# An attention with two dense stages on one core: U and V converted later, thresholds and copies of the first pair on GpSimd, steps moved within their slots

## The chip, the core and the metric

The kernel runs on one core of a Trainium2 chip. The metric is the device time of one launch in microseconds (us); three runs of the kernel before gave 829.96 to 831.2, median 830.89. Engines are named as in the profile: PE is TensorE, DVE is VectorE, ACT is ScalarE, POOL is GpSimd, SP issues transfers. All of them run their own queue in program order and wait for one another by semaphores.

## What is computed

```python
scores = scale * np.matmul(q, k.transpose(0, 1, 3, 2))          # 4 x 8 heads, 576 x 64
thresh = np.max(scores, axis=-1, keepdims=True) - tau
scores = np.where(scores >= thresh, scores, -1000000000.0)
attn = softmax(scores); x = attn @ v                            # heads side by side: 4 x 576 x 512
u = x + (x.transpose(0, 2, 1) @ U @ V).transpose(0, 2, 1)       # U 576 x 32, V 32 x 576
y = u + np.maximum(u @ w_ch1, 0.0) @ w_ch2                      # 512 x 2048 x 512
gate = 1 / (1 + np.exp(-causal_conv(y, conv_w)))                # 5 taps
out = gate * (y @ w_val) @ w_out
```

U, V, the weights and conv_w arrive as 64-bit floats and are turned into 32-bit floats on the chip, in about ten integer and float steps per block ("conversion").

## The kernel before

The 32 heads are worked in 16 pairs, and each pair in 9 slots of 128 query rows: slot 9p holds the 64 bottom query rows of both heads (the tail, through a block-diagonal tile `bd`), slots 9p+1 to 9p+8 the upper rows of one head or the other. A slot's row block goes through a pipeline: scores (TensorE, `s`, L429), their negated copy with the row minimum (VectorE, `ns` and `nm`, L443), the exponential (ScalarE, L457), the threshold `th = nm + tau` (L458), the mask (VectorE, `e`, L468, which needs `th` and runs one slot later), four transposes of `e` and every other slot a tail transpose (TensorE, `xm` L484 and `xs` L501, two or three slots later), their eviction (ScalarE, `pt` and `pk`). `pv` (L538) multiplies with v when a group of slots is complete: the first of pair p in slot 9p+8, the second in 9p+12. `back` (L548, L551) turns the result round and scales it into `ring`; `mix_t`, `mix_ut` and `mix_u` add the U and V product and write `u`.

The next pair is prepared meanwhile: `prep_T` (L356, L370) transposes q, k and the tails, ScalarE evicts a high part (L323, L325) and VectorE the rest (L329, L333) into `qk`; `stacks` copies them by transfers on SP into `st` (L383 to L391); `tails` copies the bottom query rows into `bd` on GpSimd (L401). Scores of slot 9 need `bd`, those of slots 10 and 11 the two `st`.

The order of each engine's queue is the order in which the program issues. A table `AT` (L198) says in which slot of its pair an event stands; `ORDER` sorts the TensorE events of a slot; evictions are put off with `later(slot, m, ...)` into four lists, which the main loop runs for m = 0 to 3, sorted by `LATE_ORDER`. A conversion is a generator (`from_f64` L100 to L131, with `wt` and `wf` as its tiles) that issues one step for each `work.tick()`, two blocks side by side; ticks come from `wtick` at point 3 of a slot, in every slot under 18 and then in the slots of `CONVERT_AT` (modulo 18), and in slots 2 to 7 at point 1 too. `setup_UV` (L651) converts U and V, from slot 0 on; its GpSimd work is `wf` (L131), the copy to `u4` (L657) and four `vst` (L666). `chunk` then converts the first weights, from slot 10. `load_qk` and `load_v` issue a pair's loads, two transfers per slot, in part on GpSimd's queue.

After 144 slots the dense stages follow; their first blocks (`a` L806, from `us` L786) are laced into the last slots. From the first `c` block on the kernel is a chain of matmuls.

Of the kernel before, what the change touches and what calls it, by code (L numbers as in the profile page):

```python
# [26 lines left out]
ALU = mybir.AluOpType  # L27
# [9 lines left out]
def attention_moe_kernel(  # L37
# [15 lines left out]
    nc = tc.nc  # L53
# [8 lines left out]
    NP = B * H // 2  # L62
# [6 lines left out]
    T = B * S  # L69
# [6 lines left out]
    def f(ap):  # L76
        return ap.bitcast(F32)
# [5 lines left out]
    tau_eff = const.tile([128, 1], F32, name="tau_eff")  # L83
    qscale = const.tile([128, 1], F32, name="qscale")
    cw = const.tile([128, KC, KD], F32, name="cw")
    u = const.tile([128, KD, T], F32, name="u")
# [90 lines left out]
    class Staged:  # L177
# [18 lines left out]


    AT = {  # L198
        "pv": (8, 12), "t": 15, "ut": 18, "u": 19, "Tq": -3, "Tk": 1, "Tt": 2, "stA": 4, "bd": 5, "stB": 5,
        "lq": 0, "lv": 4, "Tq1": 0,  # L200
    }

    ORDER = {
        "mix_t": 4, "mix_u": 3, "mix_ut": 5, "next_scores": 0, "prep_T": 5, "pv": 3, "back": 2,
        "trans_main": 2, "trans_tail": 2,
    }
    LATE_ORDER = {
        "T": 1, "n": -1, "nt": -2, "o": -1, "t": 0, "u": 1, "x": -2,
    }

    CONVERT_AT = (0, 1, 6, 9, 16)
    work = Staged(4)

    def scope():
# [11 lines left out]
    def attention(dense_front, dense_mid, dense_back):  # L226
# [18 lines left out]
        bd = [bd_p.tile([128, 2, 128], F32R, name=f"bd{i}") for i in range(2)]  # L245
# [40 lines left out]

        def load_v(p):
            b, h = divmod(2 * p, H)
            eng = nc.gpsimd if p < 4 else nc.sync
            eng.dma_start(  # L290
                out=vt[p % 2].rearrange("p h t d -> p h (t d)"),
                in_=v[b, h:h + 2, 0:SM, :].rearrange("h (p t) d -> p h (t d)", t=4),
            )
            yield
            for hh in range(2):
                eng.dma_start(out=vk[p % 2][hh * TL:(hh + 1) * TL, hh, :], in_=v[b, h + hh, SM:S, :])
                yield
# [15 lines left out]
        def later(s, k, fn, name=""):  # L313
            late[k].setdefault(s, []).append((LATE_ORDER.get(name, 0), fn))
# [134 lines left out]
        def soft_exp(p, i):  # L449
            d = st8[p]  # L450
            th = sm_p.tile([128, 1], F32, tag="th", name="th")
            if i == 0:
                d["e", 0] = e_p.tile([128, 2, S], F32, tag="e", name="e")
            elif i % 2:
                d["e", i] = d["e", i + 1] = e_p.tile([128, 2, S], F32, tag="e", name="e")
            nm = d.pop(("nm", i))
            nc.scalar.activation(out=row(p, i), in_=d["ns", i], func=ACTF.Exp, bias=nm[:, 0:1], scale=-1.0)  # L457
            (nc.gpsimd if p else nc.vector).tensor_tensor(out=th, in0=nm, in1=tau_eff, op=ALU.add)  # L458
            d["th", i] = th


# [79 lines left out]
        def back(s, p):  # L541
            d = st8[p]
            r = d["r"]
            x0, x = xtile("b0"), xtile("b")
            for g in (0, 1, 2):
                os = d.pop(("os", g))
                if not g:
                    nc.tensor.transpose(x0[0:TL, 0:128], os[:, 0:TL], idn)  # L548
                    continue
                for m in range(2 * g - 2, 2 * g):  # L550
                    nc.tensor.transpose(x[:, m * 128:(m + 1) * 128], os[:, m % 2 * 128:(m % 2 + 1) * 128], idn)  # L551
            rb = sm_p.tile([TL, 1], F32, tag="rb", name="rb")

            def act():
                nc.scalar.activation(out=rb, in_=r[TL:128, 0:1], func=ACTF.Copy)
                for hh, sc in ((0, r[0:TL, 0:1]), (1, rb)):
                    nc.scalar.activation(
                        out=x_of(p)[0:TL, 4, hh * D:(hh + 1) * D], in_=x0[0:TL, hh * D:(hh + 1) * D],
                        func=ACTF.Copy, scale=sc,
                    )  # L560

            later(s + 1, 0, act, "nt")
            later(s + 1, 2, lambda: nc.vector.tensor_tensor(
                out=x_of(p)[:, 0:4, :].rearrange("p t (h d) -> p (t h) d", h=2),
                in0=x.rearrange("p (t d) -> p t d", t=8),
                in1=r[:, 1:9].unsqueeze(2).to_broadcast([128, 8, D]), op=ALU.mult,
            ), "n")
# [39 lines left out]
        for hh in range(2):  # L607
            t = st8[0]["st", hh] = st_p.tile([128, 3, S], F32R, tag="st", name="st")
# [4 lines left out]
        for m in range(2):  # L613
# [7 lines left out]
            out=rv[0][:, 0:8 * R].rearrange("p (t r) -> p t r", t=4),  # L621
# [30 lines left out]
        def setup_UV(part):  # L652
            w = yield from convert(raw_uv[part])
            o = 0 if part else nu
            c, n = (FC - nu, nu + S - FC) if part else (0, FC - nu)
            if not part:
                nc.gpsimd.tensor_scalar(  # L657
                    out=u4.rearrange("p t (g r) -> p t g r", g=4),
                    in0=w[:, 0:nu].rearrange("p (t r) -> p t r", t=5).unsqueeze(2).to_broadcast([128, 5, 4, R]),
                    scalar1=1.0, scalar2=0.0, op0=ALU.mult, op1=ALU.add,  # L660
                )
            nc.scalar.activation(out=vst[:, c:c + n], in_=w[:, o:o + n], func=ACTF.Copy)
            yield
            for a in (R, 3 * R):
                lo = vst[a:a + R, c:c + n]
                nc.gpsimd.tensor_tensor(out=lo, in0=w[a:a + R, o:o + n], in1=f(lo), op=ALU.subtract)  # L666
            done.append(0)

        NS = 9 * NP + AT["ut"] - 7
        slots = [[] for _ in range(NS + 2)]  # L670
        def put(s, what, *a):
            slots[s].append((what, a))

        for p in range(NP):
            s0 = 9 * p
            for i in range(9):
                put(s0 + i + 2, trans_main, p, i)
                if i % 2 == 0:
                    put(s0 + i + 2 + (i == 8), trans_tail, p, i)
            put(s0 + AT["pv"][0], pv, p, 0, 1)  # L680
            end = p == NP - 1
            put(s0 + AT["pv"][1], pv, p, 2)
            put(s0 + AT["pv"][1] + 2, back, p)
            if p + 1 < NP:
                s1 = s0
                put(s1 + AT["Tq" if p else "Tq1"], prep_T, p + 1, "q")
                put(s1 + AT["Tk"], prep_T, p + 1, "k")
                put(s1 + AT["Tt"], prep_T, p + 1, "tail")
                put(s1 + AT["stA"], stacks, p + 1, 0)
                put(s1 + AT["bd"], tails, p + 1)  # L690
                put(s1 + AT["stB"], stacks, p + 1, 1)
            put(s0 + AT["t"], mix_t, p)
            put(s0 + AT["ut"] - end, mix_ut, p)
            put(s0 + AT["u"] - 2 * end, mix_u, p)
        def next_scores(s):
            scores(*divmod(s + 1, 9))

        last = (stacks, tails)
        work.add(setup_UV(0))
        work.add(setup_UV(1))  # L700
        scores(0, 0)
        for s in range(NS):
            p, i = divmod(s, 9)
            slot[0] = s
            live = p < NP
            ev = slots[s]
            if s == 10: chunk(0, 0)
            if s == 10: chunk(0, 1)
            work.width = 2 if s < 9 * NP - 11 else 4
            def wtick(at):  # L710
                if at == 3 and (s < 18 or s % 18 in CONVERT_AT) or at == 1 and 2 <= s < 8:
                    work.tick()
            wtick(-1)
            if live:
                soft_max(p, i)
            for m in (0, 1, 2, 3):
                for _, fn in sorted(late[m].pop(s, []), key=lambda x: x[0]):
                    fn()
                if m == 1 and live:
                    soft_exp(p, i)  # L720
                if m == 2 and 1 <= s <= 9 * NP:
                    soft_mask(*divmod(s - 1, 9))
                wtick(m)
            wtick(4)
            if s + 1 < 9 * NP:
                ev = [(next_scores, ())] + ev
            for what, a in sorted(ev, key=lambda x: 9 if x[0] in last else ORDER.get(x[0].__name__, 5)):
                what(*a) if what in last else what(s, *a)
            if i == AT["lq"] and p + 2 < NP:
                loads.append(load_qk(p + 2))  # L730
            if i == AT["lv"] and p + 1 < NP:
                loads.append(load_v(p + 1))
            load(2)
            if s == 9 * NP:
                front.close()
                ps_s.close()
            if s == 9 * NP + 1:
                mid.close()
                dense_mid()
            if s == 9 * NP + AT["pv"][1] + 2 - 9:  # L740
                top.close()
            if s >= 9 * NP:
                steps = next(dense_front, None)
                if s == 9 * NP:
                    later(s + 1, 0, lambda: list(steps))
                work.tick()
# [304 lines left out]
```

## Time and profile before

| | |
|---|---|
| median of three runs | 830.89 us |
| profiled execution | 831.23 us, span 829.5 us |
| PE (TensorE) busy | 815.3 us, 98% |
| DVE (VectorE) busy | 616.2 us, 74% |
| ACT (ScalarE) busy | 437.4 us, 53% |
| POOL (GpSimd) busy | 240.3 us, 29% |
| chain that ended last | PE 90%, ACT 4%, DMA 2%, POOL 2%, DVE 1% |

The chain is followed back from the last instruction, at each step to what released it or to the instruction ahead of it on its engine. A busy TensorE can still be slower than it need be: matmul ends are modelled, and a matmul that waits for its data inside a run of matmuls counts as busy. A share over the whole span also mixes the attention (about 324 us) with the dense stages.

### The profile page before, as it was taken

Reading aid. Unit: us, or ns where it says so; the run is one execution under the profiler, and the core shown is the slowest. Engines: PE = TensorE matmul, PEld = TensorE weight load, DVE = VectorE, ACT = ScalarE, POOL = GpSimd, SP = SyncE. Lnnn points to the kernel's source line nnn. Section 1 sums busy time; section 2 is a strip of 40 time slices with the busy share of each in tenths; the row PEclk is TensorE's granted clock in tenths of the full one; section 3 lists DMA queues with packets and bytes.
Section 4 is the critical chain, followed back from the end, with each engine's and each line's share of the span. In section 5 each row is a group of like instructions: output and inputs, shape, how many; then the busy total and the mean of one; then the engine's idle time right before and its main releaser. Section 6 shows DMA issues by size and latency. Waiting matters only on the chain.

```text
span 829.5 us, 14295 instructions
## 1 busy us (share of the span) xinstructions
PE 815.3 (98%) x5084; PEld 691.9 (83%) x5084; DVE 616.2 (74%) x1309; ACT 437.4 (53%) x894; POOL 240.3 (29%) x329
## 2 busy tenths in 40 slices
PE   8799999999999999999999999999999999999998
PEld 7688888888888887788888888888888888888886
DVE  7799898999889898356874776357743688999740
ACT  5588888888878888223333232224222334345431
POOL 6744543364334332002430352005220233200000
PEclk9999999999999999999999999999999999999999
DMA  5655586667766540001220221003110111001112
GB/s 134 166 145 130 135 197 143 148 145 171 167 145 151 147 101 27 2 18 59 76 77 1 75 77 52 1 3 101 51 51 1 52 51 51 1 1 51 51 51 76
DMA packets 63567, 68.07 MB, mean 82 GB/s; under 512 B 43349, under 2 KB 46821, under 8 KB 63498
## 3 DMA queue, kind: packets, MB, share of 16 engines
q1 hardware_dynamic: 60730, 63.68, 29.5%
q0 software_dynamic: 1424, 3.10, 1.2%
q8 instruction: 41, 0.67, 0.3%
q10 hardware_dynamic: 1344, 0.39, 0.2%
q14 instruction: 28, 0.23, 0.1%
HBM read 35.89 MB, written 4.72 MB: 49 GB/s over the span
## 4 chain that ended last, share of the span: by engine, by line
PE 90%; ACT 4%; DMA 2%; POOL 2%; DVE 1%; issue 1%; SPq 0%; ACTq 0%; DVEq 0%; POOLq 0%
PE c L806 24%; PE a L806 24%; PE s L429 8%; PE o L538 8%; PE v L806 6%; PE p L965 6%; PE xm L484 6%; PE t L577 2%; PE o L527 2%; ACT pt L493 1%; PE tm L356 1%; ACT e L457 1%; PE u L589 1%; PE xs L501 1%; DMA st<-qk 1%
## 5 line engine op out<-in xcount | busy, mean ns | idle before, releaser
L806 PE MATMUL a<-us,w 128*128 128x512 f32 (+1 forms) x960 | 202.3, 369 | 0.6 <-DVE us L786 0.6
L806 PE MATMUL c<-h,w 128*128 128x512 f32 (+1 forms) x960 | 200.7, 368 | 0.0
L806 PEld LDWEIGHTS a<-us,w 128*128 128x128 f32 x960 | 167.0, 189 | 31.5 <-DVE us L786 1.3
L806 PEld LDWEIGHTS c<-h,w 128*128 128x128 f32 x960 | 167.4, 189 | 30.0
L817 ACT ACTIVATE h<-a 128x512 fp32r<-128x512 f32 (+1 forms) x80 | 44.2, 554 | 186.9 <-PE a L806 186.9
L131 POOL TENSOR_TENSOR wf<-wf,wt 128x512 f32<-128x512 f32 (+2 forms) x43 | 58.5, 1361 | 268.2 <-DVE wt L126 268.2
L458 POOL TENSOR_TENSOR th<-nm,tau_eff 128x1 f32<-128x1 f32 x135 | 80.7, 598 | 165.9 <-DVE ns L443 164.5
L818 DVE SCALAR_TENSOR_TENSOR h<-a,h 128x512 fp32r<-128x512 f32 (+1 forms) x80 | 50.8, 636 | 103.6 <-ACT h L817 103.6
L443 DVE TENSOR_SCALAR_CACHE_REDUCE ns<-s 128x576 f32<-128x576 f32 x144 | 108.3, 752 | 19.8 <-PE s L429 19.7
L468 DVE SCALAR_TENSOR_TENSOR e<-ns,th,e 128x576 f32<-128x576 f32 x144 | 119.5, 830 | 0.7 <-ACT e L457 0.5
L457 ACT ACTIVATE e<-ns,nm 128x576 f32<-128x576 f32 x144 | 111.5, 774 | 13.3 <-DVE ns L443 12.9
L429 PE MATMUL s<-st 128*128 128x288 f32 x480 | 94.0, 318 | 0.0
L493 ACT ACTIVATE pt<-xm 128x512 f32<-128x512 f32 x144 | 85.4, 593 | 5.7 <-PE xm L484 3.1
L484 PE MATMUL xm<-idn,e 128*128 128x128 f32 x576 | 86.7, 274 | 0.7 <-DVE e L468 0.7
L429 PEld LDWEIGHTS s<-st 128*128 128x128 f32 x480 | 67.8, 189 | 11.5 <-issue 4.6
L484 PEld LDWEIGHTS xm<-idn,e 128*128 128x128 f32 x576 | 69.9, 141 | 1.6 <-ACT pk L515 0.6
L538 PE MATMUL o<-pt,vt 128*64 128x256 f32 (+1 forms) x768 | 69.8, 331 | 0.0
L538 PEld LDWEIGHTS o<-pt,vt 128*64 128x64 f32 x768 | 41.4, 137 | 24.5 <-issue 10.6
L172 POOL TENSOR_TENSOR w<-wf,w 128x512 fp32r<-128x512 f32 x36 | 54.5, 1530 | 10.0 <-ACT w L170 10.0
L871 DVE TENSOR_TENSOR y<-c,y 128x64 f32<-128x64 f32 (+4 forms) x96 | 39.8, 449 | 21.2 <-PE c L806 21.2
L894 DVE SCALAR_TENSOR_TENSOR u<-y,cw,u 128x576 f32<-128x576 f32 x64 | 55.0, 872 | 0.6
L786 DVE TENSOR_TENSOR us<-u,us 128x1024 fp32r<-128x1024 f32 (+1 forms) x42 | 47.7, 1176 | 7.2 <-ACT us L785 7.2
(122 smaller groups left out, 1035.7 us busy)
## 6 DMA issues: line engine op xcount, KB each, us to landing
raw<-in_moe_w_ch_dram SPq DMA_DIRECT2D x32, 512.0 KB, 3.9
st<-qk SPq DMA_DIRECT2D x30, 256.0 KB, 3.4
st<-qk SPq DMA_DIRECT2D x15, 432.0 KB, 4.0
st<-qk SPq DMA_DIRECT2D x45, 144.0 KB, 3.4
out_dram<-ring SPq DMA_DIRECT2D x17, 256.0 KB, 2.0
st<-qk SPq DMA_DIRECT2D x15, 288.0 KB, 4.8
kn<-in_k_dram SPq DMA_DIRECT2D x28, 128.0 KB, 3.4
qn<-in_q_dram SPq DMA_DIRECT2D x26, 128.0 KB, 3.5
```

Of the source, the lines that this page charges most:

```text
L131: nc.gpsimd.tensor_tensor(out=dst, in0=dst, in1=tf, op=ALU.add)
L172: lo_eng.tensor_tensor(out=lo, in0=w, in1=f(hi), op=ALU.subtract)
L429: nc.tensor.matmul(s[:, n, 0:HS], lhs, rhs[:, n * HS:(n + 1) * HS], start=(m == 0), stop=(m == len(ops) - 1))
L443: nc.vector.tensor_scalar(out=ns.rearrange("p (a b) -> p a b", a=2), in0=s, scalar1=-1.0, scalar2=3.0e38, op0=ALU.mult, op1=ALU.min, accum ...
L457: nc.scalar.activation(out=row(p, i), in_=d["ns", i], func=ACTF.Exp, bias=nm[:, 0:1], scale=-1.0)
L458: (nc.gpsimd if p else nc.vector).tensor_tensor(out=th, in0=nm, in1=tau_eff, op=ALU.add)
L468: nc.vector.scalar_tensor_tensor(out=e, in0=d.pop(("ns", i)), scalar=d.pop(("th", i))[:, 0:1], in1=e, op0=ALU.is_le, op1=ALU.mult, accum_o ...
L484: nc.tensor.transpose(x[:, j * 128:(j + 1) * 128], e[:, c + j * 128:c + (j + 1) * 128], idn)
L493: later(s + 1, 0, lambda: nc.scalar.activation(out=dst, in_=x.rearrange("p (j c) -> p j c", j=4), func=ACTF.Copy), "x")
L538: nc.tensor.matmul(o, lhs, rhs, start=False, stop=stop)
L806: nc.tensor.matmul(ps[:, 0:m1], lhs, rhs, start=(m == 0), stop=(m == len(ops) - 1))
L894: nc.vector.scalar_tensor_tensor(out=g, in0=y[:, e, b, k:k + S], scalar=cw[:, k, e:e + 1], in1=g, op0=ALU.mult, op1=ALU.add)
```

## The change

What it does, in the order of the diff:

- `AT`, `PREP_AT`: `back` stands in slot 13 of its pair (14 before), `mix_u` in 18 (19 before), the odd tail transpose (i = 8) a slot sooner; the `bd` copies stand in slot 4 of the pair that runs while they are prepared (5 before).
- `LATE_ORDER`: evictions of `prep_T` come first in their list (they came last, together with those of `u`).
- `CONVERT_AT`: six slots in eighteen, five before; the tick moves from point 3 of a slot (behind list 3) to point 0 (behind list 0).
- v of pairs 0 to 3 is loaded through SP, not GpSimd.
- The thresholds of pair 0 are computed on GpSimd as all others are; they were on VectorE.
- U and V enter the conversion at slot 4, not at slot 0.
- The mask is issued at the end of list 1, ahead of lists 2 and 3; `ring` moves from list 2 to list 1.

```diff
     AT = {
-        "pv": (8, 12), "t": 15, "ut": 18, "u": 19, "Tq": -3, "Tk": 1, "Tt": 2, "stA": 4, "bd": 5, "stB": 5,
-        "lq": 0, "lv": 4, "Tq1": 0,
+        "pv": (8, 12), "back": 13, "t": 15, "u": 18, "lq": 0, "lv": 4, "uv": 4, "ch": 10,
     }
+    PREP_AT = {"Tq": (-3, 0), "Tk": (1, 1), "Tt": (2, 2), "stA": (4, 4), "bd": (4, 4), "stB": (5, 5)}
...
     LATE_ORDER = {
-        "T": 1, "n": -1, "nt": -2, "o": -1, "t": 0, "u": 1, "x": -2,
+        "T": -2, "n": -1, "nt": -2, "o": -1, "t": 0, "u": 1, "x": -2,
     }
-    CONVERT_AT = (0, 1, 6, 9, 16)
+    CONVERT_AT = (0, 1, 6, 9, 12, 16)
...
         def load_v(p):
-            eng = nc.gpsimd if p < 4 else nc.sync
+            eng = nc.sync
...
-            (nc.gpsimd if p else nc.vector).tensor_tensor(out=th, in0=nm, in1=tau_eff, op=ALU.add)
+            nc.gpsimd.tensor_tensor(out=th, in0=nm, in1=tau_eff, op=ALU.add)
...
-            later(s + 1, 2, lambda: nc.vector.tensor_tensor(
+            later(s + 1, 1, lambda: nc.vector.tensor_tensor(
                 out=x_of(p)[:, 0:4, :].rearrange("p t (h d) -> p (t h) d", h=2),
...
                 if i % 2 == 0:
-                    put(s0 + i + 2 + (i == 8), trans_tail, p, i)
+                    put(s0 + i + 2, trans_tail, p, i)
...
-            put(s0 + AT["pv"][1] + 2, back, p)
+            put(s0 + AT["back"] + end, back, p)
...
-            put(s0 + AT["ut"] - end, mix_ut, p)
-            put(s0 + AT["u"] - 2 * end, mix_u, p)
+            put(s0 + AT["u"] - end, mix_ut, p)
+            put(s0 + AT["u"] - end, mix_u, p)
...
-        work.add(setup_UV(0))
-        work.add(setup_UV(1))
         scores(0, 0)
...
+            if s == AT["uv"]:
+                work.add(setup_UV(0))
+                work.add(setup_UV(1))
...
             def wtick(at):
-                if at == 3 and (s < 18 or s % 18 in CONVERT_AT) or at == 1 and 2 <= s < 8:
+                if at == 0 and (s < 18 or s % 18 in CONVERT_AT) or at == 1 and 2 <= s < 8:
                     work.tick()
...
-                if m == 1 and live:
-                    soft_exp(p, i)
-                if m == 2 and 1 <= s <= 9 * NP:
-                    soft_mask(*divmod(s - 1, 9))
+                if m == 1:
+                    if live:
+                        soft_exp(p, i)
+                    if 1 <= s <= 9 * NP:
+                        soft_mask(*divmod(s - 1, 9))
                 wtick(m)
```

The queues show what moves. In the changed file the lines from L200 on are one higher. First GpSimd (POOL), from the end of pair 2's loads to the first threshold of pair 1; `wf`, `u_120` and `vst` are the U and V conversion, `bd_126` the copies for pair 1, `th` the thresholds. Before:

```order
L281 DMA tn<-in_q_dram 64x2x64
L131 TENSOR_TENSOR wf<-wf,wt 128x512
L657 TENSOR_SCALAR u_120<-wf 128x640
L131 TENSOR_TENSOR wf<-wf,wt 128x224
L281 DMA tn<-in_k_dram 64x2x64
L290 DMA vt_130<-in_v_dram 128x2x256
L666 TENSOR_TENSOR vst<-wf,vst 32x352 x2
L666 TENSOR_TENSOR vst<-wf,vst 32x224 x2
L401 TENSOR_SCALAR bd_126<-qk 64x64 x4
L296 DMA vk_132<-in_v_dram 64x64 x2
L458 TENSOR_TENSOR th<-nm,tau_eff 128x1
```

And in the changed kernel, from the copies to threshold 10:

```order
L402 TENSOR_SCALAR bd_126<-qk 64x64 x4
L282 DMA tn<-in_k_dram 64x2x64
L459 TENSOR_TENSOR th<-nm,tau_eff 128x1 x2
L131 TENSOR_TENSOR wf<-wf,wt 128x512
L459 TENSOR_TENSOR th<-nm,tau_eff 128x1
L658 TENSOR_SCALAR u_120<-wf 128x640
L131 TENSOR_TENSOR wf<-wf,wt 128x224
L667 TENSOR_TENSOR vst<-wf,vst 32x352 x2
L459 TENSOR_TENSOR th<-nm,tau_eff 128x1
L667 TENSOR_TENSOR vst<-wf,vst 32x224 x2
L459 TENSOR_TENSOR th<-nm,tau_eff 128x1
L277 DMA qn<-in_q_dram 128x4x64 x2
```

The copies stand ahead of the conversion, and thresholds 7, 8 and 9 stand inside it; threshold 10 follows the two loads.

Second VectorE (DVE), slots 1 to 3 of pair 0. Before:

```order
L468 SCALAR_TENSOR_TENSOR e,sum<-ns,th,e 128x576
L329 SCALAR_TENSOR_TENSOR qk<-tm,qscale,qk 128x512
L105 TENSOR_SCALAR wt<-wt 128x512
L443 TENSOR_SCALAR ns,nm<-s 128x576
L458 TENSOR_TENSOR th<-nm,tau_eff 128x1
L108 TENSOR_SCALAR wt<-wt 128x512
L105 TENSOR_SCALAR wt<-wt 128x224
L468 SCALAR_TENSOR_TENSOR e,sum<-ns,th,e 128x576
L333 TENSOR_TENSOR qk<-tm,qk 128x512
L112 SCALAR_TENSOR_TENSOR wf<-raw,wt 128x512
L108 TENSOR_SCALAR wt<-wt 128x224
L443 TENSOR_SCALAR ns,nm<-s 128x576
```

And now:

```order
L469 SCALAR_TENSOR_TENSOR e,sum<-ns,th,e 128x576
L330 SCALAR_TENSOR_TENSOR qk<-tm,qscale,qk 128x512
L444 TENSOR_SCALAR ns,nm<-s 128x576
L469 SCALAR_TENSOR_TENSOR e,sum<-ns,th,e 128x576
L334 TENSOR_TENSOR qk<-tm,qk 128x512
L444 TENSOR_SCALAR ns,nm<-s 128x576
```

Thresholds and conversion steps are gone from here; the conversion steps come back between mask 3 and mask 6.

Third ScalarE (ACT), slots 16 and 17, where the first weight block (`wt<-raw`) is converted and pair 2's q is evicted (`qk<-tm`). Before:

```order
L578 ACTIVATE t_st_127<-t 128x128
L323 ACTIVATE qk<-tm,qscale 128x512
L457 ACTIVATE e<-ns,nm 128x576
L103 ACTIVATE wt<-raw 128x512
L493 ACTIVATE pt<-xm 128x4x128
```

And now:

```order
L579 ACTIVATE t_st_127<-t 128x128
L103 ACTIVATE wt<-raw 128x512
L324 ACTIVATE qk<-tm,qscale 128x512
L458 ACTIVATE e<-ns,nm 128x576
L494 ACTIVATE pt<-xm 128x4x128
```

The conversion step stands ahead of the eviction instead of behind the exponential.

## Rows read from the trace of the kernel before

**Rows 1.** Windows by stage: start and end, length, busy us of each engine, PEclk, DMA share, GB/s.

```profile
0.00:40.00 40.00, 31.71 (x231) 28.13 (x232) 29.10 (x80) 21.02 (x43) 26.52 (x48) 0.96 0.60 156
40.00:320.00 280.00, 279.01 (x2386) 239.88 (x2384) 254.66 (x678) 239.49 (x559) 116.89 (x213) 1.00 0.60 143
354.00:829.50 475.50, 471.62 (x2285) 398.69 (x2283) 315.39 (x524) 161.88 (x261) 92.73 (x65) 1.00 0.14 45
```

**Rows 2.** Timeline of TensorE, 30 to 54 us: start, length, instruction, idle before.

```profile
31.83 1.89 PE L429 MATMUL s<-qk,bd 128*128 128x288 f32 x6 [2.97 <-POOL bd L401]
...
34.58 1.10 PE L527 MATMUL o<-pk,vk 128*128 128x64 f32 x4
...
39.56 0.60 PE L484 MATMUL xm<-idn,e 128*128 128x128 f32 x4
...
41.08 0.60 PE L484 MATMUL xm<-idn,e 128*128 128x128 f32 x4
...
42.28 0.60 PE L484 MATMUL xm<-idn,e 128*128 128x128 f32 x4
...
51.66 1.04 PE L429 MATMUL s<-qk,bd 128*128 128x288 f32 x6
52.53 0.60 PE L484 MATMUL xm<-idn,e 128*128 128x128 f32 x4
...
53.08 1.10 PE L527 MATMUL o<-pk,vk 128*128 128x64 f32 x4
```

**Rows 3.** Window of 1 us behind the idle stretch, columns as in rows 1.

```profile
32.00:33.00 1.00, 1.00 (x4) 0.96 (x5) 0.00 (x0) 0.00 (x0) 0.94 (x3) 0.50 0.89 348
```

**Rows 4.** Timeline of VectorE, 20 to 40 us; then its thresholds, grouped by line.

```profile
27.47 0.75 DVE L443 TENSOR_SCALAR_CACHE_REDUCE ns<-s 128x576 f32<-128x576 f32 x1
...
28.34 0.81 DVE L468 SCALAR_TENSOR_TENSOR e<-ns,th,e 128x576 f32<-128x576 f32 x1
...
38.78 0.76 DVE L443 TENSOR_SCALAR_CACHE_REDUCE ns<-s 128x576 f32<-128x576 f32 x1 [3.06 <-PE s L429]
...
39.47 0.81 DVE L468 SCALAR_TENSOR_TENSOR e<-ns,th,e 128x576 f32<-128x576 f32 x1
...
L458 DVE TENSOR_TENSOR th<-nm,tau_eff 128x1 f32<-128x1 f32 x9 | 2.2, 242 | 0.3
```

**Rows 5.** Timeline of GpSimd, 20 to 40 us.

```profile
21.19 1.26 POOL L131 TENSOR_TENSOR wf<-wf,wt 128x512 f32<-128x512 f32 x1 [7.10 <-DVE wt L126]
...
23.33 1.15 POOL L131 TENSOR_TENSOR wf<-wf,wt 128x224 f32<-128x224 f32 x1
...
25.86 4.53 POOL L666 TENSOR_TENSOR vst<-wf,vst 32x352 fp32r<-32x352 f32 x4
...
35.28 1.56 POOL L276 DMA_DIRECT2D qn<-in_q_dram  x2
```

**Rows 6.** Thresholds on GpSimd, 30 to 320 us: shortest, median, longest in ns.

```profile
L458 POOL TENSOR_TENSOR th<-nm,tau_eff x134: 188/637/792, 34.7 to 318.2; 128x1 f32<-128x1 f32 x134
```

**Rows 7.** SP's queue, first and last stack transfer; then landing times, 0 to 50 us.

```profile
20.58 0.52 SPq L383 DMA_DIRECT2D st<-qk  x1
...
27.98 0.85 SPq L391 DMA_DIRECT2D st<-qk  x1
...
st<-qk SPq DMA_DIRECT2D x5, 144.0 KB, 4.9
```

**Rows 8.** Chain that ended last, 60 to 130 us: first `pv` of pairs 2 to 4.

```profile
73.31 2.34 PE o L538 x32
...
92.67 2.34 PE o L538 x32
...
111.77 2.34 PE o L538 x32
```

**Rows 9.** Timeline of TensorE, 324 to 333 us: the hand-over to the dense stage.

```profile
325.85 3.06 PE L806 MATMUL a<-us,w 128*128 128x512 f32 x11 [0.57 <-DVE us L786]
...
332.28 0.70 PE L527 MATMUL o<-pk,vk 128*128 128x256 f32 x2 [0.52 <-ACT pk L515]
```

More of the change, by code (lines that the diff above doesn't have):

```diff
@@ L667, in setup_UV @@
             done.append(0)
-        NS = 9 * NP + AT["ut"] - 7
-        slots = [[] for _ in range(NS + 2)]
+        NS = 9 * NP + AT["u"] - 7
+        slots = [[] for _ in range(NS + 1)]
         def put(s, what, *a):
@@ L675, in attention @@
             s0 = 9 * p
+            end = p == NP - 1
             for i in range(9):
@@ L678, in attention @@
                 if i % 2 == 0:
-                    put(s0 + i + 2 + (i == 8), trans_tail, p, i)
+                    put(s0 + i + 2, trans_tail, p, i)
             put(s0 + AT["pv"][0], pv, p, 0, 1)
-            end = p == NP - 1
             put(s0 + AT["pv"][1], pv, p, 2)
-            put(s0 + AT["pv"][1] + 2, back, p)
+            put(s0 + AT["back"] + end, back, p)
             if p + 1 < NP:
[L685 to L691, printed above, removed]
+                for name, what, *a in (("Tq", prep_T, "q"), ("Tk", prep_T, "k"), ("Tt", prep_T, "tail"),
+                                       ("stA", stacks, 0), ("bd", tails), ("stB", stacks, 1)):
+                    put(s0 + PREP_AT[name][not p], what, p + 1, *a)
             put(s0 + AT["t"], mix_t, p)
-            put(s0 + AT["ut"] - end, mix_ut, p)
-            put(s0 + AT["u"] - 2 * end, mix_u, p)
+            put(s0 + AT["u"] - end, mix_ut, p)
+            put(s0 + AT["u"] - end, mix_u, p)
         def next_scores(s):
@@ L706, in attention @@
             ev = slots[s]
-            if s == 10: chunk(0, 0)
-            if s == 10: chunk(0, 1)
+            if s == AT["uv"]:
+                work.add(setup_UV(0))
+                work.add(setup_UV(1))
+            if s == AT["ch"]:
+                chunk(0, 0)
+                chunk(0, 1)
             work.width = 2 if s < 9 * NP - 11 else 4
             def wtick(at):
-                if at == 3 and (s < 18 or s % 18 in CONVERT_AT) or at == 1 and 2 <= s < 8:
+                if at == 0 and (s < 18 or s % 18 in CONVERT_AT) or at == 1 and 2 <= s < 8:
                     work.tick()
@@ L739, in attention @@
                 dense_mid()
-            if s == 9 * NP + AT["pv"][1] + 2 - 9:
+            if s == 9 * NP + AT["back"] + 1 - 9:
                 top.close()
```

## The prediction

> **What bounds the kernel now.** I read the stage windows first. From 354 us to the end TensorE works back to back: 471.62 of 475.50 us busy, and the rest is the last output's way out. From 40 to 320 us it is busy for 279.01 of 280 us. Only the first 40 us have air: 31.71 us busy, 8.3 us idle [rows 1]. So a change to the attention's order can win some microseconds at the start, little in the middle, and what the hand-over to the dense part near 325 us loses; nothing after that.
>
> Next the TensorE timeline of the first pair [rows 2]. The scores of slot 9 (the `bd` block) start at 31.83 us after 2.97 us of waiting for GpSimd's four `bd` copies; the first `pv` follows at 34.58. The reader should set beside it the same piece one pair later: scores 51.66, transposes 52.53, `pv` 53.08. It takes 1.42 us there and 2.75 us here. The reason stands in the windows: behind the idle stretch the granted clock is 0.50, that is 1.2 in place of 2.4 GHz [rows 3]. Wait and half clock together cost 2.97 + 1.33 = 4.3 us.
>
> Then VectorE in the same stretch [rows 4]. Its rows name no wait, it works through: mask 6 ends at 28.34 + 0.81 = 29.15. The transposes of mask 6 stand right behind the `bd` scores, so without the `bd` wait VectorE would be next.
>
> **The change, part by part.** All sums are against the profiled execution, 831.23 us (span 829.5), which lies 0.34 us above the median of 830.89; I take the gain from the median.
>
> *Thresholds of pair 0 to GpSimd.* With its threshold a slot spends 28.34 - 27.47 = 0.87 us from the start of `ns` to the mask, without it 39.47 - 38.78 = 0.69 [rows 4]. Eight of the nine stand before mask 6: 8 x 0.18 = 1.4 us at least; the nine were busy for 2.2 us, since some were held up, and that is the most. I take 2.0, nearer to the busy time, which is measured in this very stretch. The conversion of U and V stays ahead of mask 6 on VectorE (it only starts at slot 4), so nothing else goes from this sum: mask 6 ends near 27.1. Transposes and tail take 53.08 - 52.53 = 0.55 us, so the first `pv` starts near 27.7 in place of 34.58: 6.9 us. That holds the 4.3 us of wait and half clock.
>
> *`bd` copies in slot 4, ahead of U and V on GpSimd.* They read the tails that VectorE evicts in slot 3, and are through well before the scores of slot 9. The wait of 2.97 us goes; its gain is in the 6.9.
>
> *What is late next: GpSimd.* In its new queue the U/V work stands between the thresholds 6 and 9, and the loads of pair 3 behind threshold 9. VectorE ends the wide `wt` some 2.0 us before mask 6 (mask 0.81, `ns` 0.69 and two narrow steps), at 25.1. From there GpSimd needs 24.48 - 21.19 = 3.29 us for both `wf` and the copy between, 4.53 us for four `vst`, 1.56 us for two loads of q, and the thresholds 7 to 10 [rows 5]. A threshold took 0.188 to 0.792 us there, median 0.637 [rows 6]. Before, TensorE came to the transposes of masks 8, 9 and 10 at 39.56, 41.08 and 42.28 us, 4.98, 6.50 and 7.70 us after `pv` [rows 2]; from 27.7 that is 32.7, 34.2 and 35.4.
> With every threshold at 0.64 us: `wf` and threshold 7 to 29.1, two `vst` to 31.4, threshold 8 to 32.0, its mask to 32.8 (0.1 late); two `vst` and threshold 9 to 34.9, mask to 35.7 (1.4 late); loads and threshold 10 to 37.1, mask to 37.9 (1.0 late). In sum 2.5 us lost.
> With thresholds 8 to 10 at 0.19 us the masks end at 32.4, 34.9 and 36.6: 0 + 0.7 + 0.5 = 1.2 us lost. VectorE waits for these thresholds with nothing to run, so the short value may well hold; but the long one is the median. I take 1.8, the middle. Start: 6.9 - 1.8 = 5.1 us.
>
> The median of 0.64 us beside a shortest of 0.19 is what a threshold shows that lies behind a mask [rows 6]. The Trainium skill, SBUF — State Buffer, section Who interferes with whom, says that a VectorE instruction with two SBUF inputs and a GpSimd instruction that reads SBUF shut each other out for the length of the one that came first. By that rule moving thresholds to GpSimd only moves the contention, but not in slots 8 to 10, where masks wait: there the short times hold, and the sum would be 7.5 us in place of 6.9. The trace agrees so far as the two durations show.
>
> *The stacks' transfers.* SP issues nine transfers from 20.58 to 28.83 us, and 144 KB took 4.9 us to land in this stretch [rows 7]. One `vt` load now stands among them; at an estimated 0.8 us (the last stack took 0.85) the last lands 8.25 + 0.8 + 4.9 = 14.0 us after the tails are evicted. The scores of slot 11, which stand right ahead of the transposes at 32.7, want it by 32. So the tails must be out by 18, 2.6 us sooner than before. Four thresholds no longer stand ahead of them (0.7 us), nor do the seven conversion steps of the first slots: I estimate 3 us together and cost this at nothing. If only the thresholds counted, it would cost 1.9 us, and that is in the range. `vt` and `vk` of pair 0 on SP: nothing, they are issued at the start.
>
> *Conversion early in a slot, `T` evictions first, `back` and `tail` a slot sooner.* Pairs alternate between 111.77 - 92.67 = 19.10 and 92.67 - 73.31 = 19.36 us [rows 8]; where it is 19.36 the chain runs through ScalarE ahead of `pv` (`qk`, exponential, a conversion step, `pt`). In the new order that conversion step stands ahead of `qk`, where ScalarE had to wait for the transposes anyway. Four or five odd pairs show it: 0.26 x 4 = 1.0 at best, nothing at worst. I take 0.8. A conversion step between `ns` and the mask delays a mask by up to a step; masks have a slot of slack there, so 0.
>
> *One more conversion slot in eighteen.* The steps of chunk 0 end before the last slots, and none is left between the last masks and `us`. TensorE waits 0.57 us for `us` at 325.85 and 0.52 us for `pk` at 332.28, which lies on ScalarE behind such a step [rows 9]. The last tail transpose also comes ahead of the `a` block now. Both can go: 1.1 at best, 0.4 if one stays; I take 1.0.
>
> Sum: 5.1 + 0.8 + 1.0 = 6.9 us. From 830.89 that gives **824.0 us**.
>
> **The rivals.** 0.2% (1.7 us) is about what a measurement of this kernel can tell from no change.
>
> *GpSimd costs nothing.* Thresholds and `vst` run at their short times, `pv` starts at 27.3 (the whole 2.2 us of thresholds saved), the odd pairs lose all their excess: 7.3 + 1.0 + 1.1 = 9.4 us, 821.5 us. For it: VectorE waits in that stretch and holds nobody up. Against: two loads of 1.56 us stand ahead of threshold 10 whatever VectorE does.
>
> *GpSimd costs more.* The `bd` copies and loads make thresholds late in slots 4 to 6 too, and the masks there lie on VectorE's full queue: 1 to 2 us more lost, odd pairs keep their excess: 6.9 - 2.0 - 0.8 = 4.1 us, 826.8 us. For it: a threshold in GpSimd's queue waits for loads of 0.78 us each. Against: a threshold has a whole slot until its mask.
>
> *The wait only moves.* In place of `bd` the scores of slot 11 wait for the stacks' transfers, or the late thresholds eat the start's gain; 5 us lost again: within 1.7 us of before, 829.2 to 832.5. Against: the transfers start with the tails, which come earlier.
>
> *Slower.* GpSimd becomes the bound from slot 7 to 11. Nine instructions (two `wf`, the copy, four `vst`, two thresholds) each wait for one more mask of 0.81 us than in their rows: 7.3 us; TensorE idles in stretches as long as the one before and drops to half clock again, 1.3 us. 6.9 - 7.3 - 1.3 = -1.7: 832.6 us. It decides from the point where GpSimd's stretch grows by 7 us. Against: masks that wait for thresholds can't hold them up as well.
>
> **How the numbers follow.** My forecast has 0.62 with its own range of 822.3 to 826.0; GpSimd for nothing 0.14; GpSimd dearer 0.14; the wait only moves 0.06; slower 0.04. The first three are all faster by over 1.7 us: 0.90. The range runs from the best case with half a microsecond of doubt, 821.0, to the dearer case with 1.2 us, 828.0.
>
> **What would show it.** Right: no `bd` wait; `pv` of pair 0 at 27 to 28.5 us; clock 1.00 from 20 to 40 us; masks 9 and 10 waiting for thresholds, 1 to 2.5 us of TensorE idle between 31 and 38 us; pair periods all near 19.1; no wait for `us` or `pk` near 325. Wrong: `pv` of pair 0 after 30 us, a wait for `st`, or a half clock anywhere.

## The result, and the profile after

The changed kernel takes **820.47 us** (median of four runs, 820.41 to 820.97), beside 830.93 us for the kernel before (829.96 to 831.2) in the same batch: 10.46 us less, ratio 0.9877 with a 95% interval of 0.986 to 0.9895. The forecast was 824.0 us with a range of 821.0 to 828.0, so the sign was right and the gain was under-sized by 3.5 us, half a microsecond beyond the range. Most runs of the kernel before lie near 829.4 or near 831.1 us, and its median moves between these from batch to batch; a gain is therefore given against the median of its own batch, and where a microsecond matters it is read from the traces.

The windows by stage of the changed kernel, columns as in [rows 1], which they answer to:

```profile
0.00:40.00 40.00, 36.47 (x281) 31.74 (x282) 34.35 (x88) 26.86 (x57) 29.47 (x61) 1.00 0.65 169
40.00:320.00 280.00, 278.23 (x2402) 240.84 (x2400) 260.37 (x679) 241.74 (x563) 101.48 (x200) 1.00 0.61 143
320.00:345.00 25.00, 25.00 (x129) 20.11 (x128) 8.42 (x12) 8.13 (x17) 0.16 (x1) 1.00 0.00 1
```

The first 40 us hold 4.8 us more of TensorE's work, and the clock is full throughout. TensorE's busy time in the middle has not risen; it has even fallen from 279.01 to 278.23 us, and yet the middle is shorter. That is the riddle of this case.

TensorE's timeline at the first pair, which answers to [rows 2]:

```profile
25.21 1.02 PE L430 MATMUL s<-qk,bd 128*128 128x288 f32 x6 [0.81 <-DVE ns L444]
26.68 0.63 PE L485 MATMUL xm<-idn,e 128*128 128x128 f32 x4 [0.45 <-DVE e L469]
27.15 0.27 PE L502 MATMUL xs<-idn,e 128*128 128x128 f32 x1
27.26 0.92 PE L528 MATMUL o<-pk,vk 128*128 128x64 f32 x4
```

The wait for `bd` is gone, the scores of slot 9 take 1.02 us and not 1.89, and the first `pv` starts at 27.26 us, 7.32 sooner than before. From there I took the start of every pair's first `pv` and that of the dense stage's `c` block, and how much sooner each comes than before: pair 0 7.32 us, pair 1 6.57, pair 5 7.38, pair 9 8.98, pair 15 8.83, the `c` block 10.45 (343.54 in place of 353.99). So 0.75 us of the start is lost in the first period, 2.3 us are won in the middle, 1.6 at the hand-over to the dense part.

### The profile page after: what moved, and what is told of

The parts are those of the page before. It is cut to its first block, busy times and chain, and to the rows that moved or that the text cites. A ratio compares the mean times of both kernels' runs of the same rounds, so it can differ in the third digit from the quotient of the medians.

```text
span 818.7 us, 14233 instructions
## 1 busy us (share of the span) xinstructions
PE 809.9 (99%) x5084; PEld 690.2 (84%) x5084; DVE 617.7 (75%) x1300; ACT 437.4 (53%) x894; POOL 223.8 (27%) x326
## 4 chain that ended last, share of the span: by engine, by line
PE 94%; DVE 2%; ACT 2%; DMA 1%; issue 1%; POOL 0%; SPq 0%; ACTq 0%; POOLq 0%; DVEq 0%
PE a L806 24%; PE c L806 24%; PE s L430 9%; PE o L539 8%; PE xm L485 7%; PE v L806 6%; PE p L965 6%; PE o L528 2%; PE t L578 2%; PE tm L357 1%; PE xs L502 1%; PE u L590 1%; DMA kn<-in_k_dram 1%; PE b L552 1%; DVE e L469 1%
## 5 line engine op out<-in xcount | busy, mean ns | idle before, releaser
L469 DVE SCALAR_TENSOR_TENSOR e<-ns,th,e 128x576 f32<-128x576 f32 x144 | 124.3, 863 | 1.5 <-POOL th L459 0.4
L459 POOL TENSOR_TENSOR th<-nm,tau_eff 128x1 f32<-128x1 f32 x144 | 72.4, 503 | 175.1 <-DVE ns L444 168.1
L172 POOL TENSOR_TENSOR w<-wf,w 128x512 fp32r<-128x512 f32 x36 | 54.0, 1514 | 10.0 <-ACT w L170 10.0
```

The lines of the kernel that those rows point to most:

```text
L172: lo_eng.tensor_tensor(out=lo, in0=w, in1=f(hi), op=ALU.subtract)
L459: nc.gpsimd.tensor_tensor(out=th, in0=nm, in1=tau_eff, op=ALU.add)
L469: nc.vector.scalar_tensor_tensor(out=e, in0=d.pop(("ns", i)), scalar=d.pop(("th", i))[:, 0:1], in1=e, op0=ALU.is_le, op1=ALU.mult, accum_o ...
```

## The experiments

Each was timed beside the kernel before in its own batch. Where a run is set against the changed kernel (820.47 us), the two medians come from different batches; the traces, given beside them where it matters, differ from that by about half a microsecond at most. "Period" is the time from one pair's first `pv` to the next pair's.

**The start alone, in the kernel before.**

```
-  eng = nc.gpsimd if p < 4 else nc.sync
+  eng = nc.sync
-  (nc.gpsimd if p else nc.vector).tensor_tensor(out=th, ...
+  nc.gpsimd.tensor_tensor(out=th, ...
-  put(s1 + AT["bd"], tails, p + 1)
+  put(s1 + (AT["bd"] if p else 4), tails, p + 1)
+  if s == 4: work.add(setup_UV(0)); work.add(setup_UV(1))
```

> The kernel before with the start alone changed: U and V converted from slot 4, the first pair's thresholds on GpSimd, the bottom queries of pair 1 copied in slot 4, the first v loads on SP. Theory A (start worth 7.3, GpSimd's late thresholds cost 0.9): 6.4 us, 824.0 to 825.0 us, the first pv near 27.3 us and pair periods 19.10 and 19.36 as before. Theory B (GpSimd's queue costs the 1.8 us that the prediction took, and the chunk's conversion steps that come sooner help the later pairs): first pv the same but over 25.5 us from it to the last pair, 825.3 to 826.3 us.

Measured: 825.90 us (825.82 to 826.82) beside 831.04, 5.1 us less. The first `pv` starts at 27.54 us, 7.04 sooner; the first period is 20.51 us and not 18.50, 2.0 us lost; the later ones are those of before (19.33, 19.10, 19.39, 19.13). Theory B's price holds, without its help to later pairs: the prediction's start, 6.9 - 1.8 = 5.1 us, is right in its sum and nearly in both terms. So the missing gain is not at the start.

The 2.0 us are not lost where the prediction put them, though, at the late masks 8 to 10. The rows of GpSimd, ScalarE (two) and TensorE show the larger part:

```profile
26.09 1.86 POOL L131 TENSOR_TENSOR wf<-wf,wt 128x512 f32<-128x512 f32 x1
27.99 0.50 ACT L662 ACTIVATE vst<-wf 128x352 fp32r<-128x352 f32 x1 [1.39 <-POOL wf L131]
28.39 0.58 ACT L493 ACTIVATE pt<-xm 128x512 f32<-128x512 f32 x1
29.02 0.70 PE L527 MATMUL o<-pk,vk 128*128 128x256 f32 x2 [1.04 <-ACT pt L493]
```

ScalarE's copy of V into `vst` waits for GpSimd's `wf`, a `pt` stands behind that copy, and TensorE stops inside the first `pv` until that `pt` is done (1.04 us under PE, 1.18 under the weight loads). By the program the first `pv` does not read this `pt`, whose rows belong to the second; so it must be the PSUM tile that it waits for, as mix_t does further down. Of the masks only one stops TensorE: mask 10, whose threshold stands behind two loads, for 0.7 us at 36.93.

**`back` in slot 13 alone, in the kernel before.**

```
-  put(s0 + AT["pv"][1] + 2, back, p)
+  put(s0 + AT["pv"][1] + 1 + end, back, p)
```

> The kernel before with one edit: the back transposes stand in slot 13 of a pair and not in slot 14 (the last pair keeps 14). Theory A: the missed microseconds in the middle are mix_t's wait of 0.28 us in each of 15 pairs, which ends with the eviction of `back`; a slot sooner it goes, so 15 x 0.28 = 4.2 us at most: 826.5 to 828.0 us, with the wait of the t weight load gone from the list of waits and periods of about 18.85 us. Theory B (the conversion steps early in a slot make the middle faster): this edit alone does nothing, 830.4 to 831.4 us.

Measured: 825.82 us (825.23 to 826.89) beside 831.04, ratio 0.9943 (0.993 to 0.9955): 5.2 us less, more than theory A allowed, and theory B falls. In the trace the periods go from 19.10 and 19.36 to 18.79 and 19.06, 0.3 us each, and from pair 0 to pair 15 it is 4.6 us; the rest of this run's gain lies ahead of the first `pv` and is told at the end. TensorE's weight loads (PEld) in pair 6 of the kernel before show what went; the columns are start, length, instruction, idle before:

```profile
163.66 0.50 PEld L484 LDWEIGHTS xm<-idn,e 128*128 128x128 f32 x4
164.12 0.14 PEld L501 LDWEIGHTS xs<-idn,e 128*128 128x128 f32 x1
164.54 1.19 PEld L577 LDWEIGHTS t<-ring,u 128*128 128x128 f32 x10 [0.28 <-ACT pt L493]
```

The first weights of mix_t wait 0.28 us. ScalarE's timeline names the place:

```profile
163.27 0.20 ACT L555 ACTIVATE rb<-r 64x1 f32<-64x1 f32 x1
163.50 0.31 ACT L557 ACTIVATE ring<-b,r 64x64 f32<-64x64 f32 x1
163.72 0.30 ACT L557 ACTIVATE ring<-b,rb 64x64 f32<-64x64 f32 x1
163.91 0.58 ACT L493 ACTIVATE pt<-xm 128x512 f32<-128x512 f32 x1
```

The three evictions of `back` stand ahead of that `pt`, which ends at 164.49; mix_t starts 0.05 us later, in this pair and in all fifteen. One line of the list of waits sums it up (total, times, longest):

```profile
PEld t L577 <- ACT pt L493: 4.3, 15, 0.3
```

In the kernel with `back` in slot 13 that line is absent, and so it is in the changed kernel, where the same piece reads:

```profile
156.26 0.14 PEld L502 LDWEIGHTS xs<-idn,e 128*128 128x128 f32 x1
156.37 1.20 PEld L578 LDWEIGHTS t<-ring,u 128*128 128x128 f32 x10
```

The window of the middle in the kernel with `back` in slot 13, to be set beside the second row of [rows 1]:

```profile
40.00:320.00 280.00, 278.97 (x2420) 241.69 (x2419) 258.57 (x683) 240.73 (x566) 120.59 (x212) 1.00 0.61 142
```

PE is busy for 278.97 us, as before for 279.01, though each pair takes 0.3 us less. In pair 6 of the kernel before the `xs` matmul ahead of mix_t counts as busy from 164.23 to 164.50 us, although its weights were in by 164.26 and mix_t's began at 164.54: the wait lies inside a busy time. Only the number of instructions (2420 in place of 2386) and PEld's busy time (241.69 in place of 239.88) say that more was done. The Trainium skill, Perfetto Trace Analysis, section Identifying the Most-Contended Engine, says that the busy share of matmuls is no measure of how near TensorE is to its limit and that of the weight loads is; these two rows agree.

**`back` put back to slot 14, in the changed kernel.**

```
-  put(s0 + AT["back"] + end, back, p)
+  put(s0 + AT["back"] + 1, back, p)
```

> The changed kernel with `back` put back to slot 14, all else as changed. Theory A: mix_t waits again, 820.5 + 3.0 to 4.2 = 823.5 to 824.7 us. Theory B: 820.0 to 821.2 us.

Measured: 825.13 us (824.87 to 825.53), 4.7 us above the changed kernel, 0.4 more than theory A allowed: its direction holds and theory B falls. mix_t waits again; most periods are 19.1 to 19.2 us in place of 18.8 to 18.9. But the 4.7 us are not that wait alone. In twelve pairs mix_t waits 0.3 to 0.4 us as before, 3.6 us in sum; in the other three it waits 0.98, 1.16 and 1.18 us, and there it is the ring that is late, since a conversion step of VectorE stands ahead of its eviction. In return three other waits of the changed kernel, told below, do not come here.

**mix_t moved away instead, in the kernel before.**

```
-  put(s0 + AT["t"], mix_t, p)
+  put(s0 + AT["t"] + 1 - end, mix_t, p)
```

> The kernel before with `back` left in slot 14 and mix_t moved from slot 15 to slot 16 instead (the last pair keeps 15). Theory A (all that counts is that a whole slot lies between the ring evictions of `back` and mix_t, so that TensorE finds ScalarE's and VectorE's evictions done): the wait of 0.28 us in 15 pairs goes here too, 4.2 to 4.6 us less than before, 825.3 to 826.8 us. Theory C (the gain came from what else moved with `back`, its ScalarE evictions ahead of other pt evictions): nothing, 829.4 to 831.3 us.

Measured: 838.80 us (837.66 to 839.2) beside 829.40, 9.4 us slower. Both expectations are wrong, and the weight loads say why. What now stands where mix_t stood, the transposes `tm` of the next queries, waits in its place:

```profile
166.57 0.14 PEld L501 LDWEIGHTS xs<-idn,e 128*128 128x128 f32 x1
167.01 0.42 PEld L356 LDWEIGHTS tm<-idn,qn 128*128 128x128 f32 x4 [0.30 <-ACT pt L493]
```

`tm` reads nothing of the ring. So the wait of the kernel before was not for the ring: it belongs to the place in the order, the third PSUM tile that is drawn in slot 15 (after `xm` and `xs`). The pool has four such tiles (L239), and the third one drawn there begins 0.05 us after ScalarE has read slot 14's `xm`, whoever draws it. That the pool hands it the very buffer of that `xm` is inferred from this; the trace names no buffers. And the next user of mix_t's own tile pays more. From the list of the weight loads' waits of this kernel:

```profile
PEld o L527 <- DVE t_st L579: 8.8, 15, 1.4
...
PEld tm L356 <- ACT pt L493: 3.8, 13, 0.3
```

`pv`, in the next slot, waits until VectorE has read t: 8.8 us in 15 pairs, where the kernel before has no such line. By the same inference moving `back` ahead is good because its two tiles are drawn and read a slot sooner: then whoever comes third in slot 15 gets a tile that was read long ago.

**The conversion steps where they were, in the changed kernel.**

```
-  CONVERT_AT = (0, 1, 6, 9, 12, 16)
+  CONVERT_AT = (0, 1, 6, 9, 16)
-  if at == 0 and (s < 18 or s % 18 in CONVERT_AT) ...
+  if at == 3 and (s < 18 or s % 18 in CONVERT_AT) ...
```

(the mask and the ring eviction also go back to the later part of the slot)

> The changed kernel with the conversion steps where they were: at the end of a slot, in five slots of eighteen, and mask and back eviction in their old part of the slot. Theory A (the steps early in a slot give the odd pairs' 0.26 us and the tail about 1.0, and cost three stretched masks of 0.57 us each): the three stalls go (-1.7), the odd pairs' excess and the tail's waits return (+2.0 to +3.0): 820.8 to 822.0 us. Theory B (they make the whole gain of the middle, 2.3 us, and the tail's 1.6): 823.5 to 825.0 us.

Measured: 821.70 us (821.19 to 821.76), 1.2 us above the changed kernel. By the trace that is three things: the first `pv` and the first period together take 48.13 us and not 46.51 (1.6 us more), from pair 1 to pair 15 it is 263.11 and not 264.46 (1.35 us *less*), and from there to the `c` block 33.44 and not 32.57 (0.9 more). So the early steps, with the sixth slot and the earlier mask and ring eviction that go with them, help at both ends and hurt in the middle. At the start ScalarE's wait for `wf`, seen in the run with the start alone, is here too (1.04 us under PE at 29.52) and is gone in the changed kernel, whose `wf` begins at 24.28 us. In the middle the excess of every other period (19.06 against 18.81) is back, as forecast; but the three long periods of the changed kernel, 19.57, 19.87 and 19.46 us (those that end with the first `pv` of pairs 4, 10 and 14), are 19.26, 18.80 and 18.56 us here.

**The ring eviction behind the mask, in the changed kernel.** In those three periods a mask takes 1.68 us. VectorE's timeline of the first of them, then GpSimd's, then TensorE's:

```profile
97.00 0.69 DVE L564 TENSOR_TENSOR ring<-b,r 128x512 f32<-128x512 f32 x1
97.60 1.68 DVE L469 SCALAR_TENSOR_TENSOR e<-ns,th,e 128x576 f32<-128x576 f32 x1
```

```profile
97.24 0.19 POOL L459 TENSOR_TENSOR th<-nm,tau_eff 128x1 f32<-128x1 f32 x1
97.38 1.28 POOL L172 TENSOR_TENSOR w<-wf,w 128x512 fp32r<-128x512 f32 x1
```

```profile
99.43 0.63 PE L485 MATMUL xm<-idn,e 128*128 128x128 f32 x4 [0.57 <-DVE e L469]
```

GpSimd's step of slot 6 waits for nothing of slot 6, so GpSimd runs ahead to it as soon as slot 5's threshold is out. Slot 5 is the one in which VectorE evicts the ring between `ns` and the mask: in that gap GpSimd begins a pass of 1.28 us, and the mask that comes 0.22 us later is held. The edit closes the gap:

```
-  later(s + 1, 1, lambda: nc.vector.tensor_tensor(
+  later(s + 1, 2, lambda: nc.vector.tensor_tensor(
       out=x_of(p)[:, 0:4, :]...
```

> The changed kernel with one instruction per pair moved on VectorE: the eviction of `back` into the ring stands behind the mask of its slot and not between `ns` and the mask. Theory A: the three masks of 1.68 us (pairs 4, 10 and 14) are held out by GpSimd's conversion step of 1.28 us, which GpSimd runs ahead to as soon as the slot's threshold is out, because the ring eviction of 0.69 us leaves it the gap; with the mask right behind `ns` they go back to 0.81 and the periods of 19.57, 19.87 and 19.46 us to about 18.85: 0.72 + 1.02 + 0.61 = 2.3 us less, 818.0 to 818.9 us. Theory B: the masks are long because VectorE's own conversion steps crowd slot 6; moving the ring eviction does nothing, 820.1 to 821.0 us.

Measured: **818.25 us** (818.04 to 818.73) beside 829.87, ratio 0.9856 (0.9841 to 0.987): 2.2 us under the changed kernel, with no run in common, and the fastest here. By the traces the `c` block comes 1.8 us sooner: 2.3 us are won between pair 1 and pair 15, and 0.5 are lost ahead of the first `pv`. Theory A holds. The three periods are 18.84, 19.13 and 18.62 us, and the same place reads, VectorE and GpSimd:

```profile
97.47 0.81 DVE L469 SCALAR_TENSOR_TENSOR e<-ns,th,e 128x576 f32<-128x576 f32 x1
98.21 0.09 DVE L469 DVE_READ_ACCUMULATOR e<-ns,th,e 128x1 f32 x1
98.21 0.69 DVE L564 TENSOR_TENSOR ring<-b,r 128x512 f32<-128x512 f32 x1
```

```profile
97.71 0.62 POOL L459 TENSOR_TENSOR th<-nm,tau_eff 128x1 f32<-128x1 f32 x1
98.29 1.29 POOL L172 TENSOR_TENSOR w<-wf,w 128x512 fp32r<-128x512 f32 x1
```

Now the mask comes first and the threshold waits behind it, 0.62 us in place of 0.19; the pass runs beside the ring eviction, which takes 0.69 us as ever. That is the rule of the Trainium skill that the prediction quoted (SBUF — State Buffer, Who interferes with whom) in both orders: a mask, with two inputs in SBUF, and a GpSimd pass hold each other out, and whoever starts first keeps the other waiting; the ring eviction, one of whose inputs lies in PSUM, is not held.

**The step moved instead of the eviction.** Slot 6 of the table changed to 7, and in a second kernel to 3; nothing else:

```
-  CONVERT_AT = (0, 1, 6, 9, 12, 16)
+  CONVERT_AT = (0, 1, 7, 9, 12, 16)
```

> The changed kernel with the conversion step of slot 6 in slot 7 of eighteen. Theory A (as above: only the slot behind the ring eviction is a bad place): the three stalls go, 818.0 to 819.3 us, unless the step in slot 7 delays the pt evictions ahead of pv in slot 8, which the even pairs would show as 0.25 us each, 819.5 to 820.5 us. Theory B (a conversion step early in a slot stretches a mask wherever it stands): masks over 1.2 us in another slot and 820.2 to 821.5 us.

> The changed kernel with the conversion step of slot 6 in slot 3 of eighteen, where TensorE runs the second pv of an odd pair (1.95 us). Theory A: no held masks and no excess of the odd periods, 818.0 to 818.9 us. Theory B (a step stretches a mask wherever it stands): 820.2 to 821.5 us.

Measured: 819.95 us (819.91 to 820.34) with slot 7 and 821.46 us (821.42 to 821.73) with slot 3. The three long masks are gone in both, as theory A says, but other waits come: with slot 7 two masks near the end of the attention are late (TensorE idle for 0.32 us at 292.65 and 0.51 at 310.33), with slot 3 one is late by 1.11 us at 311.44, and two transposes wait 0.26 us each for `back`'s evictions. What makes these masks late are VectorE's own conversion steps between `ns` and the mask (L172 and L126, 0.7 us each, with slot 7; two of L172, 1.29 us together, with slot 3). So neither pair of expectations is met whole: 819.95 us lies in theory A's second range without the 0.25 us in the even pairs that were its reason, and 821.46 us is theory B's time without its stretched masks. A moved step brings waits elsewhere; in the kernel with the moved eviction TensorE has no wait of 0.2 us or more after 37 us, as PE counts them.

**Thresholds of pair 0 back on VectorE, in the changed kernel.**

```
-  nc.gpsimd.tensor_tensor(out=th, ...
+  (nc.gpsimd if p else nc.vector).tensor_tensor(out=th, ...
```

> The changed kernel with the nine thresholds of pair 0 back on VectorE. By the prediction's price they take 1.4 to 2.2 us from VectorE ahead of mask 6, so the first pv starts at 28.6 to 29.5 us and not at 27.26; GpSimd's queue then has no thresholds between U and V, and the 0.9 us by which masks 9 and 10 came late there comes back at most: 820.9 to 821.8 us. Rival, after the rule that the two engines shut each other out on SBUF: on GpSimd the thresholds only moved the contention, so it makes no difference, 820.2 to 820.8 us.

Measured: 821.60 us (821.45 to 821.81), 1.1 us above the changed kernel. The first `pv` starts at 29.15 us, 1.89 later (the prediction took 2.0), and the first period is 0.85 us shorter, since GpSimd's queue is. The rival falls: the first `pv` shows that the thresholds did cost VectorE what they took. By the traces the `c` block comes 1.06 us later than in the changed kernel.

**U and V later.** With the ring eviction behind the mask, slot 4 became 6 and 8:

```
-  "uv": 4,
+  "uv": 6,
```

> The changed kernel with the ring eviction behind the mask, and U and V converted from slot 6 and not from slot 4. Theory A: TensorE's waits of 0.82, 0.45 and 0.23 us between 25 and 37 us come from VectorE's conversion steps and GpSimd's vst passes there; two slots later they meet pv's 3.2 us, and half to all of 1.5 us goes: 816.7 to 817.6 us. Theory B (the work only moves on to the masks of pair 1): 818.0 to 819.2 us.

> As the run before, with U and V converted from slot 8. Theory A: the first pv comes up to a microsecond sooner than 27.75 and nothing is late behind it: 816.5 to 817.6 us. Theory B: U, V and with them the first weight chunk come two more slots late, mix_t of slot 15 waits for u4 or the tail for the weights: 818.5 to 821.0 us.

Measured: 820.43 us (820.35 to 820.52) and 825.14 us (824.65 to 825.24), 2.2 and 6.9 us above the version with slot 4. The first `pv` does come sooner, at 25.59 and 25.75 us in place of 27.75, but the first period grows from 19.23 to 22.29 and 21.31 us, and with slot 8 five of the later periods are 0.4 to 0.8 us longer and the way from the last `pv` to the `c` block 33.98 us in place of 32.59. Theory A falls in both. Theory B has the direction, but both runs are slower than it allowed (819.2 and 821.0 us at most). With slot 6 TensorE waits 1.24 us for `ns` at 32.77 and 0.74 for a mask at 41.69, which is the work moved on; with slot 8 it waits 1.36 us for a mask at 42.23 and 0.99 for `us` at 322.00, but mix_t does not wait for `u4`.

**Without the added conversion slot**, again with the ring eviction behind the mask:

```
-  CONVERT_AT = (0, 1, 6, 9, 12, 16)
+  CONVERT_AT = (0, 1, 6, 9, 16)
```

> The changed kernel with the ring eviction behind the mask and without the added conversion slot 12 of eighteen. By the prediction the added slot lets the chunk's steps end before the last masks and so takes TensorE's waits for `us` and `pk` away: without it they return, 0.5 to 1.1 us, 818.8 to 819.4 us. Rival: the tail's gain comes from the earlier tail transpose and the earlier steps alone, and a step less in eighteen slots frees the masks: 817.5 to 818.4 us.

Measured: 820.14 us (819.92 to 820.29), 1.9 us slower than with it by the medians and 1.5 by the traces, more than expected: 0.6 us behind the last `pv`, where a wait for `us` is back (0.4 us under PE), 0.7 in the last period and 0.7 in the period that ends with pair 12, less what a few other periods gain. The wait for `pk` does not return. The rival falls.

## Why the prediction was wrong, and where it was right

Four of the kernels make a chain, each adding one part of the change, and their medians show where the gain of 10.5 us came from (the last of them is from another batch):

| from | to | gain, us | forecast |
|---|---|---|---|
| before, 831.04 | start alone, 825.90 | 5.1 | 5.1 |
| start alone, 825.90 | with `back` and the odd tail transpose sooner, `u` beside `ut`, `T` evictions first, `bd` copies in slot 4 in all pairs, 821.70 | 4.2 | part of 1.8 |
| 821.70 | with early conversion steps, slot 12, mask and ring eviction sooner: the change, 820.47 | 1.2 | the rest of 1.8 |

**The start held in its sum, in part by luck.** The first `pv` was forecast at 27.7 us and came at 27.26 in the change and 27.54 alone. The half clock is gone. GpSimd's queue was forecast to cost 1.8 us through late masks, and alone it cost 2.0. But 1.2 of these came by a path that the prediction did not have, ScalarE's copy that waits for `wf` with a `pt` behind it, and 0.7 by mask 10, which it had. In the change the first period loses only 0.75 us: it also holds `back`'s gain, and that path is gone with the early conversion steps (first period 20.08 us with the steps late, 19.25 with them early). The thresholds that waiting masks wanted took the short time, as the second of the two sums supposed. From GpSimd's timeline of the changed kernel:

```profile
27.82 2.34 POOL L667 TENSOR_TENSOR vst<-wf,vst 32x352 fp32r<-32x352 f32 x2
30.24 0.19 POOL L459 TENSOR_TENSOR th<-nm,tau_eff 128x1 f32<-128x1 f32 x1
30.51 1.80 POOL L667 TENSOR_TENSOR vst<-wf,vst 32x224 fp32r<-32x224 f32 x2
32.39 0.19 POOL L459 TENSOR_TENSOR th<-nm,tau_eff 128x1 f32<-128x1 f32 x1
```

**The step that failed** is the paragraph "Conversion early in a slot, `T` evictions first, `back` and `tail` a slot sooner". It gave the four edits one price of 0.8 us, the odd periods' excess, and `back` nothing, because the first paragraph had read "little in the middle" from 279.01 us of 280 in [rows 1]. `back` alone is worth 4.6 us by the trace in the kernel before (putting it back into slot 14 of the change costs 4.7, of another make-up): the list of waits of the kernel before had the line of 4.3 us in 15 waits, but under the weight loads, and I had looked for waits under PE. Had the sum held it, it would have stood at 819.4 us. With it the periods are near 18.8 us and not near 19.1, which the prediction gave as a sign of being right.

**In the same paragraph the 0.8 us was near**, and "masks have a slot of slack there, so 0" was wrong the other way. The excess of every other period is about 0.25 us with the steps late and mostly under 0.1 with them early; from pair 1 to pair 15 the kernel with the late steps takes 263.11 us and the one with early steps and the ring eviction behind the mask 262.18, 0.9 less (slot 12 is in that difference too). But three masks are held for 0.87 us each, and these cost 2.2 us, which the run with the ring eviction behind the mask gives back. The two errors have opposite signs, 4.6 us too little and 2.2 too much, and partly hid each other: with both the sum would stand at 821.6 us, and the last microsecond lies in the first period and the hand-over, which were better than forecast. The `T` evictions first swap two neighbours on VectorE; no run tried them by themselves, nor `u` beside `ut`.

**The hand-over** was forecast at 1.0 and gave 1.6 us. As PE counts, TensorE waits neither for `us` nor for `pk` in the changed kernel [rows 9]; under the weight loads there was more to win, and a part is left. The lists of waits before (two lines) and after:

```profile
PEld a L806 <- DVE us L786: 1.3, 2, 0.9
PEld o L527 <- ACT pk L515: 0.9, 1, 0.9
PEld a L806 <- DVE us L786: 0.4, 1, 0.4
```

Some 0.7 us come with the second step of the chain, in which the wait for `pk` is gone, and 0.9 with the early steps and slot 12, which take the longer of the two waits for `us`.

**The rivals.** "GpSimd costs nothing" named 821.5 us, near the result, but for the wrong reason: GpSimd's queue did cost two microseconds by itself, and still 0.75 in the change. Nothing of "the wait only moves" or "slower" came: the stacks' transfers are never waited for.

## What to carry to other kernels

Where a stage is called full because PE is busy, read the waits of the weight loads too: some 0.3 us ahead of one load in each of 15 pairs were 4.6 us here, and PE's busy time did not move when they went. When steps that draw from a small pool of PSUM tiles change places, ask which tile comes third or fourth after them and who read it last, since the wait stays with the place and not with the instruction. And where GpSimd's passes share a stretch with VectorE's two-input instructions, leave no gap ahead of a mask that TensorE waits for; put what must stand between behind it.

## What was not expected of the hardware

The same four `bd` copies, at the same place of an unchanged queue, took 1.61 us in the trace of the kernel before and 1.08 us in that of the kernel with `back` in slot 13, whose order up to there is the same:

```profile
30.49 1.61 POOL L401 TENSOR_SCALAR bd<-qk 64x64 fp32r<-64x64 f32 x4
30.47 1.08 POOL L401 TENSOR_SCALAR bd<-qk 64x64 fp32r<-64x64 f32 x4
```

The first `pv` starts at 34.58 us in the one and at 32.91 in the other, 1.67 us apart, which is also the distance between the two values near which most runs of the kernel before lie. In the first trace a mask of VectorE starts among the copies, at 30.86 us, and one copy takes 0.76 us where the median is 0.24; in the second that mask starts at 31.59, behind them. The kernel with mix_t moved has the second order too (1.08 us, first `pv` at 32.65). I take it that these are the two outcomes of one race, of the copies with a mask on VectorE, followed by TensorE's half clock behind its idle stretch [rows 3]; no run tried that by itself, and that the two values are these two outcomes is not shown. The changed kernel, which has no wait there, runs within 0.6 us.
